# A fused attention and two-MLP kernel: seven products instead of eight in one more stage, and an issue order for the sums at the end of attention

## Chip, cores and metric

One core of one Trainium2 chip. The metric is the device time of one execution in microseconds (us). Five engines are spoken of: PE (TensorE; its weight loads are a row of their own, PEld), DVE (VectorE), ACT (ScalarE), POOL (GpSimd), and SP, which issues the DMAs.

## The reference

Clustered attention feeds an MLP with a squared ReLU, and that feeds a second MLP with a gated activation. There are 1536 tokens (2 batches of 768), model width 512, inner width 2048.

```python
x = attention(q, k, v, centroids)          # 8 heads of 64, softmax within equal clusters
h = np.maximum(x @ w1_in, 0.0);  x = (h * h) @ w1_out
h = x @ w2_in;  out = (h * np.clip(h + 3.0, 0.0, 6.0) / 6.0) @ w2_out
```

## The kernel before

Every product runs in a split form: an operand x is held as hi (rounded to fp32r) and lo = x - hi, and x @ w is three matmuls, hi·hi, hi·lo and lo·hi. ACT makes hi by a copy, DVE or POOL makes lo by a subtraction.

**Attention** is laid out by hand: a table of places says between which tiles each step stands. Its last steps, `emit_norm`, transpose the reciprocal sums on PE (tile `tn`), multiply on DVE (`xx`, L881), round on POOL (`xh<-xx`, L306) and subtract on POOL (`xl<-xx,xh`, L886). `XH` and `XL` then hold the first MLP's input. Near the end the first token block's hidden layer is already computed (tiles `h`, `rg`, `g`).

**The MLPs** are a list of operations with costs; a planner (`Plan.emit`) picks their order engine by engine from due times. The list and the attention are two hand-ordered parts, and the framework merges them: an operation of the MLP whose inputs are ready can be issued in the middle of the end of attention, as the first `token_sums` are.

The hidden dimension is cut into 8 stages of 512 columns, `st` 0 to 7; stages 4 to 7 are the second MLP. From stage 1 on a stage has four turns (pr, p): a token pair pr (two chunks c of 384 tokens) by a weight half p. A turn is a `quad`, which makes four 128x384 blocks of the hidden layer, with three groups of output matmuls of an earlier chunk between its products, and then the rest of that chunk's output matmuls. Turn 4:00 below is stage 4, pr 0, p 0; it carries the output matmuls of stage 3's last chunk. Turns 3:11, 4:00, 4:01 and 4:10 follow each other.

A plain quad takes four products of two terms, 4 x 12 = 48 matmuls. A seven-product quad (Strassen's scheme in Winograd's form) takes 7 x 6 = 42. It needs sums of the tokens (`token_sums`: u1 to u4, then hi and lo of T2, T3, T4 and of u1, which takes the place of XH, XL of chunk c1), sums of the weights (`weights_in`: 4 combinations on POOL, L1108, and 5 splits of 256 columns instead of one of 512) and sums of the results: three copies from bank to SBUF on ACT (`keep`, L1247) and three additions on DVE (`plus`, L1251). All sums of the tokens are recorded at one line (L1161 before, L1163 after), by turns on DVE and POOL.

In before, stages 1, 2, 3, 5, 6 and 7 use seven products and stage 4 uses eight: the sums of the second MLP's input are made during stage 4. PE's order within the MLPs is that of the list.

Names in the rows: banks `b_4179`, `b_4183`, `b_4187`, `b_4191` are a, b, d, e of `quad`; `b_4195`, `b_4199`, `b_4203` are the output banks; `w_68` and `s_4155` are the two weight sets, `s_4163` and `w_4119` the output weights, `wr` the raw weights (L1051 clamps them), `g_4171` (T2, T3 of pair 0), `gB` (T4), `acc` the accumulator, in which the u's are made in place.

Of the kernel before, what the change touches and what calls it, by code (L numbers as in the profile page):

```python
# [13 lines left out]
ALU = mybir.AluOpType  # L14
# [108 lines left out]
E_XL = "p"  # L123
# [128 lines left out]
def span(name, lo, n):  # L252
    return [(name, c) for c in range(lo // 16, -(-(lo + n) // 16))]
# [3 lines left out]
def cluster_attention_mlp_kernel(  # L257
# [17 lines left out]
    nc = tc.nc  # L275
# [4 lines left out]
    NT = B * S  # L280
    R = S // P
    NJ = H // 2
    HS = S // 2
# [9 lines left out]
    XH = xp.tile([P, NJ, NT], F32R, name="xh")  # L293
    XL = xp.tile([P, NJ, NT], F32R, name="xl")

    def f(ap):
        return ap.bitcast(F32)
# [7 lines left out]
    def pool_round(dst, src):  # L305
        nc.gpsimd.tensor_scalar(dst, src, 1.0, 0.0, op0=ALU.mult, op1=ALU.add)  # L306
# [69 lines left out]
    with ExitStack() as actx:  # L376
# [379 lines left out]
        U_t = {}  # L756
# [113 lines left out]
        def emit_norm(u, half):  # L870
            b, j = units[u]
            rb = rows.pop((u, half))
            t = ps_t.tile([P, 512], F32, tag="t", name="tn")
            for c in range(3):
                nc.tensor.transpose(
                    t[:, c * P : (c + 1) * P], rb[:, c].rearrange("p i d -> p (i d)"), ident
                )
            hs = slice(half * HS, half * HS + HS)
            xs = slice(b * S + half * HS, b * S + half * HS + HS)
            xx = sm_p.tile([P, HS], F32, tag="xx", name="xx")  # L880
            nc.vector.tensor_tensor(xx, t[:, :HS], U_t[u][:, hs], op=ALU.mult)  # L881
            if E_XH == "p":
                pool_round(XH[:, j, xs], xx)
            else:
                nc.scalar.activation(XH[:, j, xs], xx, AF.Copy)
            (nc.gpsimd if E_XL == "p" else nc.vector).tensor_sub(XL[:, j, xs], xx, f(XH)[:, j, xs])  # L886

        early = [None, {}]

        def emit_early(fb, part):  # L890

# [84 lines left out]
    with ExitStack() as mctx:  # L976

        def static(name, n, dt):
            pool = mctx.enter_context(tc.tile_pool(name=name, bufs=1, reuse_waits="tile"))
            return pool.tile([P, n], dt, name=name)  # L980

        TT = 384
        tmp = static("tmp", 5 * TT, F32)
# [4 lines left out]
        acc_f = static("acc", 4 * NT, F32)  # L988
# [11 lines left out]
        NS = FF // FQ  # L1000
        acc = acc_f.rearrange("p (d t) -> p d t", d=4)
        acc1 = acc_f.rearrange("p (b n) -> p b n", n=DM)
        plan = Plan()
        K0, K1 = slice(0, 2), slice(2, 4)
# [14 lines left out]
        def cols(c):  # L1019
            return slice(c * TT, c * TT + TT)  # L1020
# [4 lines left out]
        def ak(ds, c):  # L1025
            return [k for d in range(ds.start, ds.stop) for k in span("acc", d * NT + c * TT, TT)]
# [3 lines left out]
        for st in range(1, 2 * NS):  # L1030
            m, fq = divmod(st, NS)
# [122 lines left out]
        def both(name, o, x, y, ko, kx, ky):  # L1154
            plan_op = {"sub": ("tensor_sub",), "add": ("tensor_add",)}[name][0]
            eng = T_ENG[0]
            T_ENG.append(T_ENG.pop(0))
            e, cost = (nc.gpsimd, {"POOL": 1.08}) if eng == "p" else (nc.vector, {"DVE": 0.75})

            def half(d):  # L1160
                plan.add(cost, lambda: getattr(e, plan_op)(o[:, d], x[:, d], y[:, d]), kx + ky, ko)  # L1161

            half(0)  # L1163
            half(1)

        def token_sums(m, n):
            c0, c1 = 2 * n, 2 * n + 1
            t2, t3, t4 = T2[n], T3[n], T4[n]

            def part(ds, c):  # L1170
                return acc[:, ds, cols(c)], ak(ds, c)

            def sub(o, x, y):
                both("sub", o[0], x[0], y[0], o[1], x[1], y[1])

            if m == 0:
                def whole(o, ds, c):
                    both("add", o[0], f(XH)[:, ds, cols(c)], f(XL)[:, ds, cols(c)], o[1],
                         xk("XH", ds, c), xk("XL", ds, c))

                u1, u2, u3, u4 = part(K0, c1), part(K1, c1), part(K0, c0), part(K1, c0)
                whole(u2, K1, c1)
                whole(u1, K0, c1)
                sub(u3, u2, u1)
                whole(u4, K0, c0)
                sub(u1, u1, u4)
                sub(u2, u2, u1)
                whole(u4, K1, c0)
                sub(u4, u4, u2)
            else:  # L1190
                u4, u2, b11, u3 = part(K1, c0), part(K1, c1), part(K0, c0), part(K0, c1)
                if n == 0:
                    u1 = tmp[:, : 2 * TT], [("x", 0), ("x", 1)]
                else:
                    u1 = acc_f[:, 3 * NT : 3 * NT + 2 * TT], span("acc", 3 * NT, 2 * TT)
                u1 = u1[0].rearrange("p (d t) -> p d t", d=2), u1[1]
                sub(u1, u3, b11)
                sub(u3, u2, u3)
                sub(u2, u2, u1)
                sub(u4, u4, u2)  # L1200

            def final(hi, lo, x, hk, lk):
                act(0.92, lambda: nc.scalar.activation(hi, x[0], AF.Copy), x[1], hk)
                both("sub", lo, x[0], f(hi), lk, x[1], hk)

            final(t3.hi, t3.lo, u3, t3.hk, t3.lk)
            final(t2.hi, t2.lo, u2, t2.hk, t2.lk)
            final(t4.hi, t4.lo, u4, t4.hk, t4.lk)
            return lambda: final(
                XH[:, K0, cols(c1)], XL[:, K0, cols(c1)], u1, xk("XH", K0, c1), xk("XL", K0, c1)  # L1210
            )
# [11 lines left out]
        xs = [tmp[:, TT * i : TT * i + TT] for i in range(3)]  # L1223
# [193 lines left out]
        def run(groups):  # L1417
            for g in groups:
                g()
# [75 lines left out]
        for fb in range(NF):  # L1495
            del G[1, fb], G[2, fb]

        laters = []
        for st in range(1, 2 * NS):
            m, fq = divmod(st, NS)  # L1500
            seven = fq > 0

            def turn_of(pr, p, groups, st_out, c):
                some = iter(groups[:3])
                quad(m, pr, p, seven, lambda: next(some)())
                run(groups[3:])
                freed(c)

            weights_in(0, seven)
            if st == 1:  # L1510
                groups = out_groups(0, 3)
            else:
                groups = out_groups(st - 1, 3)
            turn_of(0, 0, groups, st - 1, 3)
            if st == NS:
                laters.append(token_sums(1, 0))
                laters.append(token_sums(1, 1))
            weights_in(1, seven)
            for fb in range(NF):
                weights_out(st, fb)  # L1520
            turn_of(0, 1, out_groups(st, 0), st, 0)
            if laters:
                laters.pop(0)()
            turn_of(1, 0, out_groups(st, 1), st, 1)
            turn_of(1, 1, out_groups(st, 2), st, 2)
            if laters:
                laters.pop(0)()
        run(out_groups(2 * NS - 1, 3))

        with tc.manual_schedule():  # L1530
# [35 lines left out]
```

## Time and profile before

| | us |
|---|---|
| median of 3 runs | 779.55 (778.71 to 780.35) |
| the profiled execution, its own time | 780.98 |
| its span, first to last instruction | 779.2 |
| PE busy | 758.9 (97%) |
| DVE busy | 595.7 (76%) |
| ACT, POOL busy | 498.8, 435.9 |

Attention runs from 0 to about 276, the MLPs from there to the end. The two stretches that the change touches are the seam at 260 to 320 and stage 4 with the turn ahead of it, 497 to 580. A row of the timeline has the start, the length, the engine, the line, the operation with out<-in, and in brackets the engine's idle time just before it and what ended that. A length can hold a wait for a memory port, so a row of the same shape may differ in length. PE's matmuls overlap: the spacing of starts is the rate.

### The profile page before, as it was taken

How to read it: one execution, taken by the hardware profiler on the slowest of the kernel's cores; microseconds unless marked ns; L12 is line 12 of the kernel's file. 1: busy time of each engine (PE TensorE's matmuls, PEld its weight loads, DVE VectorE, ACT ScalarE, POOL GpSimd, SP SyncE). 2: the span in 40 equal slices, each digit the busy share in tenths (PEclk: the TensorE clock that was granted, in tenths of full speed). 3: DMA queues.
4: the chain of work that ended last, by engine and by line, in shares of the span. 5: the costliest groups of instructions: out<-in, count | busy, mean ns of one | idle time of the engine just before them, and what ended most of it. 6: DMA issues, size and time to landing. Idle time of an engine off the chain costs nothing.

```text
span 779.2 us, 12856 instructions
## 1 busy us (share of the span) xinstructions
PE 758.9 (97%) x4402; PEld 716.1 (92%) x4402; DVE 595.7 (76%) x1047; ACT 498.8 (64%) x1059; POOL 435.9 (56%) x544
## 2 busy tenths in 40 slices
PE   7999999999999899999999999999999999999998
PEld 5889999999988799999999999999999889988997
DVE  6789999999998679777768776799546876776444
ACT  4889899998997555774554645655566555464331
POOL 1568788788786758972641643568473164155000
PEclk9899999999999999999999999999999999999999
DMA  8758737638432022231222123122112212300112
GB/s 182 162 113 187 162 87 157 154 82 173 106 75 68 2 63 74 77 113 55 68 95 83 55 63 99 55 66 72 55 55 81 82 55 58 104 28 28 41 40 82
DMA packets 61792, 67.35 MB, mean 86 GB/s; under 512 B 41152, under 2 KB 41408, under 8 KB 61728
## 3 DMA queue, kind: packets, MB, share of 16 engines
q1 hardware_dynamic: 61728, 66.54, 32.5%
q8 instruction: 35, 0.57, 0.3%
q14 instruction: 29, 0.24, 0.1%
HBM read 43.02 MB, written 3.15 MB: 59 GB/s over the span
## 4 chain that ended last, share of the span: by engine, by line
PE 83%; ACT 6%; DVE 6%; DMA 2%; issue 2%; POOL 2%; ACTq 0%; POOLq 0%; SPq 0%; DVEq 0%
PE b L1263 27%; PE b L1379 17%; PE b L1340 15%; PE a L834 7%; PE t L807 6%; PE s L774 3%; PE s L771 3%; ACT e L791 2%; PE tsim L563 2%; PE tq L518 1%; ACT mt L636 1%; DMA op<-HL 1%; DVE acc L1161 1%; ACT eh L817 1%; ACT et L303 1%
## 5 line engine op out<-in xcount | busy, mean ns | idle before, releaser
L807 PE MATMUL t<-ident,e 128*128 128x128 f32 x576 | 94.6, 278 | 7.8 <-ACT e L791 7.0
L1068 POOL TENSOR_TENSOR s<-wt,s 128x512 fp32r<-128x512 f32 (+1 forms) x64 | 66.6, 1051 | 51.3 <-ACT s L1066 42.8
L780 DVE TENSOR_REDUCE nm<-s 128x1 f32<-128x768 f32 x96 | 90.8, 946 | 3.4 <-PE s L774 2.6
L1251 DVE TENSOR_TENSOR b<-b,tmp 128x384 f32<-128x384 f32 x72 | 40.8, 566 | 68.0 <-PE b L1263 36.4
L807 PEld LDWEIGHTS t<-ident,e 128*128 128x128 f32 x576 | 71.6, 142 | 20.0 <-ACT e L791 10.7
L791 ACT ACTIVATE e<-s,nm 128x768 f32<-128x768 f32 x96 | 86.3, 899 | 3.6 <-DVE nm L780 3.2
L1051 POOL TENSOR_SCALAR wr<-wr 128x512 f32<-128x512 f32 x60 | 40.8, 681 | 82.2 <-DMA wr<-in_moe_w_in_dram 51.1
L1247 ACT ACTIVATE tmp<-b 128x384 f32<-128x384 f32 x72 | 35.4, 492 | 79.8 <-PE b L1263 79.7
L815 POOL TENSOR_TENSOR el<-et,eh 128x384 fp32r<-128x384 f32 x80 | 81.9, 1023 | 6.7
L1263 PE MATMUL b<-xh,w 128*128 128x384 f32 x256 | 74.3, 336 | 0.0
L1263 PE MATMUL b<-xh,s 128*128 128x384 f32 x256 | 74.3, 336 | 0.0
L834 PE MATMUL a<-eh,vs 128*128 128x384 f32 x192 | 70.6, 368 | 3.2 <-DVE u L848 3.2
L818 DVE TENSOR_TENSOR el<-t,eh 128x384 fp32r<-128x384 f32 x112 | 61.4, 551 | 15.6 <-ACT eh L817 14.2
L1068 POOL TENSOR_TENSOR w<-wt,w 128x256 fp32r<-128x256 f32 (+1 forms) x44 | 40.8, 938 | 56.2 <-ACT w L1066 47.0
L306 POOL TENSOR_SCALAR eh<-et 128x384 fp32r<-128x384 f32 x80 | 42.5, 532 | 50.1 <-ACT et L303 47.0
L834 PE MATMUL a<-el,vs 128*128 128x384 f32 x192 | 65.3, 340 | 0.0
L817 ACT ACTIVATE eh<-t 128x384 fp32r<-128x384 f32 x112 | 54.8, 491 | 12.3 <-PE t L807 10.6
L1238 ACT ACTIVATE tmp<-b,three 128x384 f32<-128x384 f32 x64 | 37.2, 581 | 35.3 <-DVE b L1251 20.6
L771 PE MATMUL s<-op 128*128 128x384 f32 x192 | 57.5, 382 | 0.0
L1379 PE MATMUL b<-s,gA 128*128 128x512 f32 (+1 forms) x234 | 56.1, 382 | 0.0
L1340 PE MATMUL b<-gA,s 128*128 128x384 f32 x276 | 54.2, 334 | 0.0
L1055 DVE TENSOR_SCALAR b<-wr 128x512 int32<-128x512 int32 x60 | 41.3, 688 | 15.2 <-ACT wr L1054 14.6
(213 smaller groups left out, 2135.4 us busy)
## 6 DMA issues: line engine op xcount, KB each, us to landing
wr<-in_moe_w_out_dram SPq DMA_DIRECT2D x32, 512.0 KB, 3.3
op<-HL SPq DMA_DIRECT2D x84, 192.0 KB, 4.6
wr<-in_moe_w_in_dram SPq DMA_DIRECT2D x28, 512.0 KB, 3.6
rawv<-in_v_dram SPq DMA_DIRECT2D x16, 192.0 KB, 3.7
out_dram<-acc SPq DMA_DIRECT2D x11, 256.0 KB, 2.1
rawq<-in_q_dram SPq DMA_DIRECT2D x14, 192.0 KB, 4.4
rawk<-in_k_dram SPq DMA_DIRECT2D x14, 192.0 KB, 3.9
wr<-in_moe_w_in_dram SPq DMA_DIRECT2D x8, 256.0 KB, 2.9
```

The costliest lines, as they stand in the source:

```text
L771: nc.tensor.matmul(s[:, h, :HS], o[:, 0, rs], o[:, 2, hs], start=True, stop=False)
L780: nc.vector.tensor_reduce(nm, S_t[n][:, :, :HS], axis=AX.XY, op=ALU.max, negate=True)
L791: nc.scalar.activation(e, s[:, :, :HS], AF.Exp, bias=nm, accum_out=sums[u][:, i * R + r : i * R + r + 1])
L807: nc.tensor.transpose(t[:, c, :], E_t[n][:, half, c * P : (c + 1) * P], ident)
L815: nc.gpsimd.tensor_sub(el, et, f(eh))
L817: nc.scalar.activation(eh, t, AF.Copy)
L818: nc.vector.tensor_sub(el, t, f(eh))
L834: nc.tensor.matmul(a[:, :HS], vs[:, kr, i, :], x[:, kr, :], start=(kr == 0 and x is eh), stop=(kr == R - 1 and x is el),)
L1068: pool(n / 365, lambda: nc.gpsimd.tensor_sub(lo, x, f(hi)), k + hk, lk)
L1263: nc.tensor.matmul(h, w[:, a, cc], x[b][:, cc], start=(first and n == 1), stop=(n == 6 * len(terms)), skip_group_check=not first,)
L1340: nc.tensor.matmul(o, x[:, ds], y, start=(fb == 0 and k == 0), stop=(fb == NF - 1 and k == 2))
L1379: nc.tensor.matmul(o, g[:, ts], w[:, ns], start=(fb == 0 and k == 0), stop=(fb == NF - 1 and k == 2),)
```

## The change

Stage 4 takes seven products (`seven = True` in every stage). `token_sums(1, 0)`, of chunks 0 and 1, is listed at the end of stage 3 (behind turn 3:11), `token_sums(1, 1)` behind turn 4:00; before, both stood there and their last step, u1 into XH and XL, came behind later quads. u1 is now made in place in `acc` and no longer in a tile of its own. Every sum of tokens gets an issue order: it stands behind the last `xx` on DVE, or behind the last `xl<-xx,xh` on POOL.

```diff
-            nc.vector.tensor_tensor(xx, t[:, :HS], U_t[u][:, hs], op=ALU.mult)
+            ending["DVE"] = nc.vector.tensor_tensor(xx, t[:, :HS], U_t[u][:, hs], op=ALU.mult)
...
-            (nc.gpsimd if E_XL == "p" else nc.vector).tensor_sub(XL[:, j, xs], xx, f(XH)[:, j, xs])
+            ending["POOL"] = nc.gpsimd.tensor_sub(XL[:, j, xs], xx, f(XH)[:, j, xs])
...
+            def emit(d):
+                with tc.issue_after(ending["DVE" if e is nc.vector else "POOL"].ins):
+                    getattr(e, plan_op)(o[:, d], x[:, d], y[:, d])
...
-                u4, u2, b11, u3 = part(K1, c0), part(K1, c1), part(K0, c0), part(K0, c1)
...
-                sub(u1, u3, b11)
+                u4, u2, u1, u3 = part(K1, c0), part(K1, c1), part(K0, c0), part(K0, c1)
+                sub(u1, u3, u1)
...
-            seven = fq > 0
+            seven = True
...
             if st == NS:
-                laters.append(token_sums(1, 0))
-                laters.append(token_sums(1, 1))
+                token_sums(1, 1)()
...
-            if laters:
-                laters.pop(0)()
+            if st == NS - 1:
+                token_sums(1, 0)()
```

The order of SP's DMAs is the same in both. POOL at the seam, before: four sums stand between the last steps of attention (`g`, `eh`, `el`, then `xh`, `xl` of the last normalisation).

```order
L1051 TENSOR_SCALAR wr_4147<-wr_4147 128x512
L1161 TENSOR_TENSOR acc<-xh,xl 128x384 x2
L1051 TENSOR_SCALAR wr_4151<-wr_4151 128x512
L306 TENSOR_SCALAR g_3716<-rg 128x384
L1161 TENSOR_TENSOR acc<-xh,xl 128x384 x2
L306 TENSOR_SCALAR eh<-et 128x3x128
L815 TENSOR_TENSOR el<-et,eh 128x3x128
L306 TENSOR_SCALAR xh<-xx 128x384
L886 TENSOR_TENSOR xl<-xx,xh 128x384
L306 TENSOR_SCALAR xh<-xx 128x384
L886 TENSOR_TENSOR xl<-xx,xh 128x384
```

POOL at the seam, after.

```order
L1052 TENSOR_SCALAR wr_4147<-wr_4147 128x512
L306 TENSOR_SCALAR g_3716<-rg 128x384
L306 TENSOR_SCALAR eh<-et 128x3x128
L815 TENSOR_TENSOR el<-et,eh 128x3x128
L306 TENSOR_SCALAR xh<-xx 128x384
L886 TENSOR_TENSOR xl<-xx,xh 128x384
L306 TENSOR_SCALAR xh<-xx 128x384
L886 TENSOR_TENSOR xl<-xx,xh 128x384
L1163 TENSOR_TENSOR acc<-xh,xl 128x384 x2
L1052 TENSOR_SCALAR wr_4151<-wr_4151 128x512
L1163 TENSOR_TENSOR acc<-xh,xl 128x384 x2
```

The four sums and one clamp of raw weights have moved behind the last `xl`.

DVE at the seam, after; `u` is the last addition of attention, `xx` its normalisation, `b` and `g` the gating of the first hidden blocks.

```order
L881 TENSOR_TENSOR xx<-tn,u 128x384 x2
L1163 TENSOR_TENSOR acc<-xh,xl 128x384
L1236 TENSOR_TENSOR b_4179<-tmp,b_4179 128x384
L1163 TENSOR_TENSOR acc<-xh,xl 128x384
L1243 TENSOR_TENSOR g_4139<-b_4179,g_4139 128x384
L1236 TENSOR_TENSOR b_4183<-tmp,b_4183 128x384
L1163 TENSOR_TENSOR acc<-xh,xl 128x384
```

The first `acc<-xh,xl` here stood ten rows ahead of `xx` before; the other rows are in their old order, and nothing else of DVE moved until stage 3.

ACT where turn 3:11 ends and 4:00 begins, before: `xh<-acc` are the input's hi parts, `tmp<-b_4179,three` the gate of the first block of stage 4.

```order
L1066 ACTIVATE s_4155<-wt_4175 128x512
L1355 ACTIVATE xh<-acc 128x384 x4
L1238 ACTIVATE tmp<-b_4179,three 128x384
L1242 ACTIVATE s_4159<-b_4179 128x384
L1203 ACTIVATE g_4171<-acc 128x768
L1238 ACTIVATE tmp<-b_4183,three 128x384
L1054 ACTIVATE wr_4151<-wr_4151 128x512
L1242 ACTIVATE gB<-b_4183 128x384
L1238 ACTIVATE tmp<-b_4187,three 128x384
L1203 ACTIVATE g_4171<-acc 128x768
```

ACT at the same place, after.

```order
L1203 ACTIVATE g_4171<-acc 128x768
L1067 ACTIVATE s_4155<-wt_4175 128x512
L1355 ACTIVATE xh<-acc 128x384 x3
L1203 ACTIVATE gB<-acc 128x768
L1247 ACTIVATE tmp<-b_4179 128x384
L1067 ACTIVATE w_68<-wt_4127 128x256
L1247 ACTIVATE tmp<-b_4187 128x384
L1067 ACTIVATE s_4163<-wt_4123 128x512
L1355 ACTIVATE xh<-acc 128x384
```

T3's and T2's hi parts (`g_4171<-acc`) now stand ahead of turn 4:00, and T4's (`gB<-acc`) directly ahead of the first `keep` (`tmp<-b_4179`), which empties bank a.

## Rows read from the trace of the kernel before

**Rows 1.** Waits of PE, 255 to 330: waiter, releaser, us in total, times, longest.
```profile
PE a L834 <- DVE u L848: 3.2, 1, 3.2
```

**Rows 2.** Stretches: length, busy (count) of PE, PEld, DVE, ACT, POOL, PE clock, DMA.
```profile
497.66:513.26 15.60, 15.60 (x92) 15.60 (x91) 10.93 (x20) 9.68 (x20) 9.13 (x10) 1.00 0.11 35
513.26:529.93 16.67, 16.67 (x98) 16.67 (x97) 15.57 (x26) 10.20 (x19) 12.43 (x14) 1.00 0.31 94
529.93:546.61 16.68, 16.68 (x85) 15.14 (x85) 15.49 (x24) 10.55 (x19) 14.89 (x14) 1.00 0.21 65
563.28:579.92 16.64, 16.64 (x85) 15.16 (x85) 8.00 (x14) 10.54 (x21) 10.37 (x14) 1.00 0.19 64
579.92:595.55 15.63, 15.63 (x80) 14.13 (x79) 9.78 (x18) 10.33 (x21) 8.77 (x11) 1.00 0.17 47
```

**Rows 3.** Chain that ended last, in order of time: start, us, engine, tile, line, count.
```profile
271.74 3.01 PE a L834 x12
...
513.26 2.08 PE b L1263 x12
```

**Rows 4.** Timeline of POOL at the seam.
```profile
265.53 1.98 POOL L1161 TENSOR_TENSOR acc<-xh,xl 128x384 f32<-128x384 f32 x2
...
268.19 0.51 POOL L306 TENSOR_SCALAR g<-rg 128x384 fp32r<-128x384 f32 x1
268.67 2.26 POOL L1161 TENSOR_TENSOR acc<-xh,xl 128x384 f32<-128x384 f32 x2
...
283.75 1.29 POOL L1068 TENSOR_TENSOR s<-wt,s 128x512 fp32r<-128x512 f32 x1 [3.66 <-ACT s L1066]
```

**Rows 5.** Timeline of ACT at the seam: the input of `g`.
```profile
265.18 0.53 ACT L365 ACTIVATE rg<-rg 128x384 f32<-128x384 f32 x1
```

**Rows 6.** Timeline of DVE at the seam.
```profile
268.74 1.34 DVE L370 TENSOR_TENSOR g<-rg,g 128x384 fp32r<-128x384 f32 x1 [4.27 <-POOL g L306]
270.00 1.01 DVE L818 TENSOR_TENSOR el<-t,eh 128x384 fp32r<-128x384 f32 x2
271.04 0.55 DVE L848 TENSOR_TENSOR u<-a,tmp 64x384 f32<-64x384 f32 x1
...
275.93 1.02 DVE L881 TENSOR_TENSOR xx<-tn,u 128x384 f32<-128x384 f32 x2
...
277.33 1.28 DVE L1161 TENSOR_TENSOR acc<-xh,xl 128x384 f32<-128x384 f32 x1
...
286.39 0.55 DVE L1243 TENSOR_TENSOR s<-b,s 128x384 fp32r<-128x384 f32 x1
```

**Rows 7.** Timeline of PE behind its wait: full spacing again, and its next wait.
```profile
276.86 0.33 PE L1438 MATMUL b<-xl,w 128*128 128x384 f32 x1
...
287.00 0.45 PE L1438 MATMUL b<-xh,w 128*128 128x384 f32 x1 [0.27 <-DVE s L1243]
```

**Rows 8.** Stretches behind PE's wait, columns as in rows 2.
```profile
274.50:275.60 1.10, 1.10 (x7) 1.07 (x6) 0.25 (x1) 0.49 (x1) 0.00 (x0) 0.50 0.00 0
276.80:278.00 1.20, 1.20 (x9) 1.20 (x8) 1.20 (x3) 0.49 (x1) 1.12 (x2) 1.00 0.00 0
```

**Rows 9.** Timeline of DVE: a sum of tokens with POOL idle.
```profile
313.25 0.55 DVE L1161 TENSOR_TENSOR acc<-xh,xl 128x384 f32<-128x384 f32 x1
```

**Rows 10.** Groups by shape, 497 to 640: count, busy, mean ns of one, idle before.
```profile
L1247 ACT ACTIVATE tmp<-b 128x384 f32<-128x384 f32 x15 | 7.4, 492 | 12.3 <-PE b L1263 12.3
L1108 POOL TENSOR_TENSOR wt<-wt,wt 128x256 f32<-128x256 f32 x10 | 7.4, 738 | 0.5
L1068 POOL TENSOR_TENSOR w<-wt,w 128x256 fp32r<-128x256 f32 x10 | 7.2, 738 | 2.2 <-ACT w L1066 2.2
L1068 POOL TENSOR_TENSOR w<-wt,w 128x512 fp32r<-128x512 f32 x4 | 5.2, 1297 | 5.7 <-ACT w L1066 5.7
L1203 ACT ACTIVATE gB<-acc 128x768 fp32r<-128x768 f32 x2 | 1.7, 836 | 0.0
```

**Rows 11.** Timeline of POOL in turn 3:10's end: the lo parts of chunk 1.
```profile
495.77 4.13 POOL L1356 TENSOR_TENSOR xl<-acc,xh 128x384 fp32r<-128x384 f32 x4 [1.31 <-ACT xh L1355]
```

More of the change, by code (lines that the diff above doesn't have):

```diff
@@ L885, in emit_norm @@
                 nc.scalar.activation(XH[:, j, xs], xx, AF.Copy)
-            (nc.gpsimd if E_XL == "p" else nc.vector).tensor_sub(XL[:, j, xs], xx, f(XH)[:, j, xs])
+            ending["POOL"] = nc.gpsimd.tensor_sub(XL[:, j, xs], xx, f(XH)[:, j, xs])
         early = [None, {}]
+        ending = {}
         def emit_early(fb, part):
@@ L1158, in both @@
             e, cost = (nc.gpsimd, {"POOL": 1.08}) if eng == "p" else (nc.vector, {"DVE": 0.75})
+            def emit(d):
+                with tc.issue_after(ending["DVE" if e is nc.vector else "POOL"].ins):
+                    getattr(e, plan_op)(o[:, d], x[:, d], y[:, d])
             def half(d):
-                plan.add(cost, lambda: getattr(e, plan_op)(o[:, d], x[:, d], y[:, d]), kx + ky, ko)
+                plan.add(cost, lambda: emit(d), kx + ky, ko)
             half(0)
@@ L1190, in token_sums @@
             else:
-                u4, u2, b11, u3 = part(K1, c0), part(K1, c1), part(K0, c0), part(K0, c1)
[L1192 to L1196, printed above, removed]
-                sub(u1, u3, b11)
+                u4, u2, u1, u3 = part(K1, c0), part(K1, c1), part(K0, c0), part(K0, c1)
+                sub(u1, u3, u1)
                 sub(u3, u2, u3)
@@ L1496, in cluster_attention_mlp_kernel @@
             del G[1, fb], G[2, fb]
-        laters = []
         for st in range(1, 2 * NS):
             m, fq = divmod(st, NS)
-            seven = fq > 0
+            seven = True
             def turn_of(pr, p, groups, st_out, c):
@@ L1521, in cluster_attention_mlp_kernel @@
             turn_of(0, 1, out_groups(st, 0), st, 0)
-            if laters:
-                laters.pop(0)()
             turn_of(1, 0, out_groups(st, 1), st, 1)
             turn_of(1, 1, out_groups(st, 2), st, 2)
-            if laters:
-                laters.pop(0)()
+            if st == NS - 1:
+                token_sums(1, 0)()
         run(out_groups(2 * NS - 1, 3))
```

## The prediction

> **What bounds the kernel now.** I read the waits of PE first, then the busy time by stretch, the chain, and last the timelines of the two places that the change touches. From the seam on, PE is the bound: in the turns around stage 4 it is busy for the whole of every stretch (15.60 of 15.60, 16.67 of 16.67) [rows 2], so a matmul that is left out there comes off the end of the kernel, unless something new makes PE wait. At the seam PE has one long wait, 3.2 us for the addition `u` on DVE [rows 1]. The other engines have room on the average but not everywhere: DVE is busy 15.57 of 16.67 in turn 4:00 and 15.49 of 16.68 in 4:01 [rows 2]. These two turns are where the change puts new work.
>
> **Part 1: 24 matmuls fewer.** Stage 4 has four quads, and each loses 48 - 42 = 6 matmuls. Twelve take 2.08 us [rows 3], so 24 take 4.16. A second reading: a turn of stage 4 takes 16.64, a turn of stage 5, which has the same output work and seven products, 15.63 [rows 2]; four times the difference is 4.04. I take 4.1.
>
> What seven products cost beside PE, for each quad: three `plus` on DVE at 0.55, the length of the addition `u` of the same width (1.65) [rows 6], and three `keep` at 0.49 on ACT [rows 10], which has some 6 us free in each turn [rows 2]. For each weight half, POOL gets four combinations at 0.738 and five lo parts at 0.738 in place of one at 1.297, 5.3 more [rows 10]. The sums of tokens are the same in number on each engine as before, but their deadline is a stage earlier: T3 of pair 0 is read by the second product of turn 4:00, where nothing of stage 4 needed a sum before.
>
> **Part 2: the seam.** POOL's row explains PE's wait. `g` starts at 268.19, though its input `rg` landed at 265.18 + 0.53 = 265.71 [rows 4, 5]: two sums and a clamp stood ahead of it. DVE, in its own order, stood still 4.27 us for `g` [rows 6], then did two `el` and `u`, and PE started at 271.74 [rows 3]. With the sums behind `xl`, `g` can start at 265.75 and end at 266.26. DVE's `g` then takes 0.85 to 1.34 (1.34 is the row beside POOL's sum, 0.85 an estimate of it undisturbed), the two `el` 1.0 and `u` 0.55 [rows 6], and PE starts 0.15 later, as before: 268.8 to 269.3, so 2.4 to 2.9 earlier. `eh` on POOL follows `g` after its own input and isn't last. A wait of about 0.8 stays.
>
> The wait has a second price. At 274.5 to 275.6 PE's granted clock is 0.50, the lower of its two levels (1.2 GHz), and at 276.8 it is 1.00 again [rows 8]; PE had been idle for over 3 us ahead of that. The twelve matmuls behind the wait took 3.01 instead of 2.08 [rows 3]. If the short wait leaves the clock up, `xx` on DVE, which follows these matmuls, comes 0.9 earlier still: 3.3 to 3.8 in all. PE itself would be 4.2 ahead by 276.86: 2.4 or more, and from 271.74 to 276.86 (5.12 us) [rows 3, 7] sixteen matmuls at 0.173 (2.77) and six short transposes, which I estimate at 0.6, leave 1.75 that is the clock's.
>
> But PE can't keep 4.2. Its next wait, at 287.00, is for DVE's `s`, which ends at 286.94 [rows 6, 7], and the stretch of DVE from `xx` (275.93) to there is one row of work without a gap; PE waited only 0.27, so it is the tighter of two about equal chains. DVE starts it 3.3 to 3.8 earlier and does one more operation in it, the sum that stood before attention's end: 0.55 alone [rows 9], 1.28 beside POOL's `xl` [rows 6]. So 2.0 to 3.2 arrive, and PE waits more at that point than before, by about 1.5. POOL's four sums (1.98 + 2.26) and the clamp fall into its idle 3.66 us ahead of 283.75 [rows 4]; they overrun it by some 0.3 once everything has moved up, which the next DMA landing absorbs. From there to the first stage the rows are in their old order and move up together. I take **2.7**; the ends are 1.1 (the clock falls all the same, and the moved sum is at its longest: 2.4 - 1.28) and 4.2 (DVE doesn't hold PE).
>
> **Part 3: new waits at stage 4.** No row of before shows PE waiting there, so this is bounded. Over turns 3:11, 4:00 and 4:01 DVE is busy 10.93 + 15.57 + 15.49 = 42.0 [rows 2]. Two seven-product quads add 3.3: 45.3, in a time that shrinks from 48.95 to 46.9. POOL has 9.13 + 12.43 + 14.89 = 36.45 [rows 2], and 10.7 more for the two weight halves is 47.1 of 46.9. POOL is full, then; what saves it is that the last sums are only read 2.6 us or more into turn 4:10, and that some clamps can stand later.
>
> Of the single deadlines the tightest is on ACT. T4's hi part now stands directly ahead of the first `keep` of turn 4:00. It waits for POOL's sum u4, and PE's third product needs the `keep`. That product comes 1.04 + 1.04 + 0.52 = 2.6 after 513.26 (six matmuls, six and a group of three, at 0.173), so u4 is due at 2.6 - 0.84 - 0.49 = 1.3 into the turn, 514.5 (0.84 and 0.49 for the two copies [rows 10]). POOL's row from 495.77 [rows 11] to the second half of u4 holds four `xl`, two lo of u1, two of T2, four sums, all at 1.03 (a quarter of 4.13), and five pieces at 0.738: 12.4 + 3.7 = 16.1, so 511.9 without a wait, and about 513 with the 1 us of waits for ACT that I find in its order. There is 1.5 of slack. DVE's deadlines (T3's lo, then T4's) come out 2 us early, and the later ones about 1. I take **0.6** for what slips, between 0 and the whole 4.1. Below nothing it can't go: PE is busy all through these turns.
>
> A row shows what can stretch all this. A sum on DVE takes 0.55 with POOL idle and 1.28 beside a POOL instruction [rows 6, 9]. The Trainium skill, in "SBUF — State Buffer", section "Who interferes with whom", says that a DVE instruction with two SBUF inputs and a GpSimd instruction that reads SBUF block each other, the second waiting for the first's whole length. The trace agrees (1.28 is below 0.55 + 1.03). By that rule a fuller POOL makes the sums on DVE longer, which speaks against this change; it is the second rival.
>
> **The sum.** Against the profiled execution's own 780.98: - 4.1 - 2.7 + 0.6 = 774.8. That execution lies 1.43 above the median of the timed runs, 779.55, so the forecast is **773.3**.
>
> **The rivals.**
> 1. PE keeps the whole of the seam: DVE's stretch turns out shorter because its sums no longer meet POOL's, and no new wait comes. - 4.2 - 4.1 gives 772.7, as a median 771.2. Against it: DVE's row has no gap to give.
> 2. The memory port. In the three turns DVE does 16 half sums and lo parts of tokens. If all meet POOL (1.28) and not half of them (0.92), DVE has 16 x 0.36 = 5.8 more, of which its spare 1.5 takes some: 4.3 reach PE, and the stage gives nothing. 780.98 - 2.7 - 4.1 + 4.3 = 778.5, as a median 777.0. For it: DVE at 97%. Against it: not every late row of DVE holds PE.
> 3. The change doesn't do at the seam what it says: the sums move, but DVE's continuous row to 287 is as long as before with one more sum in it, or PE's wait passes to another input. Only part 1 with its slip: 780.98 - 4.1 + 0.6 = 777.5, as a median 776.0. Against it: the input `rg` is there 2.5 before `g` starts.
> 4. Slower: POOL becomes the bound of turns 3:11 to 4:10. Its 47.1 is counted with mean lengths. If they are 20% longer because DVE holds the port, 56.5 against 46.9 makes u4, T2 and the weights' lo parts 9.6 late: 780.98 - 6.8 + 9.6 = 783.8, as a median 782.4. It decides from 6.8 us late, that is from lengths 14% over the means. Against it: the means are already from busy stretches.
>
> **How the numbers follow.** Forecast 0.60, rival 1 0.12, rival 2 0.13, rival 3 0.10, rival 4 0.05. The forecast's own terms reach from 771.2 (4.2 + 4.16) to about 775.5 (1.1 and 0.6 slipped); with rival 3 and the near side of rival 2 the range is 771.2 to 776.8. A measurement can tell some 0.2%, 1.6 us, from no change, so faster means below 778.0: all cases but rival 4 and the far side of rival 2. Faster 0.90, same 0.05, slower 0.05.
>
> **What would show it.** Right: PE's wait for `u` shrinks to about 0.8 and the clock stays 1.00 behind it; a new wait of 1 to 2 us on DVE comes near 284; the first quad of stage 1 starts 2.7 earlier; the turns of stage 4 take 15.6 each, with no PE wait over 0.5. Wrong: PE waits for DVE `plus` or ACT `keep` in 4:00 and 4:01 (rival 2), waits that end with POOL (rival 4), or an `xx` that isn't earlier (rival 3).

## The result, and the profile after

The changed kernel takes 773.12 us (median of six runs, 772.24 to 773.31); the kernel before, run beside it, 779.94 (778.71 to 780.38). The ratio is 0.9913, with a 95% interval of 0.9901 to 0.9926. The forecast was 773.3, and faster. The profiled execution of after took 772.61 by its own time and has a span of 770.8; that of before 780.98 and 779.2.

The waits of PE in the stretch from 255 to 340, as in [rows 1]: engine, what waited, what released it, us in total, times, longest.

```profile
PE b L1438 <- DVE s L1243: 2.1, 1, 2.1
PE a L834 <- DVE u L848: 0.2, 1, 0.2
```

Before has three waits under 0.5 there that [rows 1] does not show. One is the 0.27 for `s` in [rows 7]; the other two, behind it, are these:

```profile
PE b L1340 <- ACT acc L1350: 0.4, 1, 0.4
PE b L1462 <- ACT acc L1471: 0.3, 1, 0.3
```

The wait of 3.2 us for `u` has shrunk to 0.2, and that for DVE's `s`, the lo part of the first MLP's third hidden block, has grown from 0.27 to 2.1. The two for ACT's copies are gone. From 480 to 600 the trace lists no wait of PE at all. There the stretches by turn, columns as in [rows 2], in the order 4:00, 4:01, 4:10, 4:11 and last 3:11:

```profile
509.11:524.73 15.62, 15.62 (x91) 15.62 (x91) 12.35 (x23) 12.38 (x26) 14.53 (x19) 1.00 0.14 38
524.73:540.38 15.65, 15.65 (x80) 14.11 (x79) 14.52 (x24) 10.35 (x19) 15.62 (x15) 1.00 0.31 98
540.38:556.00 15.62, 15.62 (x79) 14.12 (x79) 10.66 (x19) 9.47 (x18) 4.86 (x6) 1.00 0.01 2
556.00:571.61 15.61, 15.61 (x80) 14.13 (x79) 10.25 (x19) 10.83 (x23) 9.80 (x13) 1.00 0.32 100
493.50:509.11 15.61, 15.61 (x92) 15.61 (x91) 13.12 (x23) 10.42 (x22) 15.45 (x17) 1.00 0.11 35
```

Every turn of stage 4 lasts 15.6 instead of 16.7 [rows 2], and PE is busy throughout. POOL is busy 15.62 of 15.65 in turn 4:01 and 15.45 of 15.61 in 3:11: it is nearly as full as forecast, and PE does not notice.

At the seam, POOL's and DVE's rows (start, length, engine, line, operation, in brackets the idle time ahead and what ended it), to be read beside [rows 4, 6]:

```profile
263.94 0.51 POOL L306 TENSOR_SCALAR g<-rg 128x384 fp32r<-128x384 f32 x1 [0.25 <-ACT rg L365]
...
274.53 2.30 POOL L1163 TENSOR_TENSOR acc<-xh,xl 128x384 f32<-128x384 f32 x2
276.92 0.65 POOL L1052 TENSOR_SCALAR wr<-wr 128x512 f32<-128x512 f32 x1
```
```profile
264.49 0.56 DVE L370 TENSOR_TENSOR g<-rg,g 128x384 fp32r<-128x384 f32 x1 [1.86 <-POOL g L306]
...
270.24 1.02 DVE L881 TENSOR_TENSOR xx<-tn,u 128x384 f32<-128x384 f32 x2
271.18 0.62 DVE L1163 TENSOR_TENSOR acc<-xh,xl 128x384 f32<-128x384 f32 x1
...
278.31 0.70 DVE L1056 TENSOR_SCALAR b<-wr 128x512 int32<-128x512 int32 x1 [0.79 <-ACT wr L1055]
...
281.77 0.55 DVE L1243 TENSOR_TENSOR s<-b,s 128x384 fp32r<-128x384 f32 x1
```

POOL starts `g` 0.07 after the end of `rg` (263.34 + 0.53) where it was 2.5 after it (0.25 is POOL's own idle time ahead of `g`), and DVE's idle time ahead of its own `g` falls from 4.27 to 1.86. DVE's row from `xx` to `s` was without a gap before [rows 6]; now it has one of 0.79. DVE's `g` itself takes 0.56 instead of 1.34; before has as short a one for an earlier block:

```profile
252.83 0.56 DVE L370 TENSOR_TENSOR g<-rg,g 128x384 fp32r<-128x384 f32 x1 [0.47 <-POOL g L306]
```

The chain of work that ended last (start, us, engine, tile, line, count) says what the gap is made of:

```profile
266.71 2.35 PE a L834 x12
...
274.53 2.30 POOL acc L1163 x2
...
276.92 0.66 POOL wr L1052
...
277.60 0.68 ACT wr L1055
...
278.31 0.71 DVE b L1056
...
281.77 0.56 DVE s L1243
```

The twelve matmuls take 2.35 where they took 3.01 [rows 3], and the granted clock is 1.00 from 264 to 282: it held there. But the chain then passes through the two sums that the change put behind `xl`, since the second clamp of raw weights stands behind these on POOL; ACT scales what was clamped, DVE decodes it, and `s` stands behind the decoding. The prediction had this clamp in POOL's idle time.

For all further comparisons I use two marks that every profile has: the start of attention's last `rg` on ACT, and the start of stage 1's first lo part on DVE. For before and for after:

```profile
336.52 0.56 DVE L1243 TENSOR_TENSOR s<-b,w 128x384 fp32r<-128x384 f32 x1
```
```profile
263.34 0.53 ACT L365 ACTIVATE rg<-rg 128x384 f32<-128x384 f32 x1
...
332.37 0.56 DVE L1243 TENSOR_TENSOR s<-b,w 128x384 fp32r<-128x384 f32 x1
```

From the second mark to the end of the span before has 779.2 - 336.52 = 442.68 and after 770.8 - 332.37 = 438.43. The difference, 4.25, is what 24 matmuls take (4.16 by [rows 3]). Between the marks ("the seam") before has 336.52 - 265.18 = 71.34 [rows 5] and after 69.03, so 2.31 less. The remaining 1.84 of the 8.4 between the spans lies ahead of the first mark, in attention, where the change has nothing; run e11 below shows what 1.1 of it was.

### The profile page after: what moved, and what is told of

It reads as the page before. It is cut to its first block, busy times and chain, and to the rows that moved or that the text cites. A ratio compares the mean times of both kernels' runs of the same rounds, so it can differ in the third digit from the quotient of the medians.

```text
span 770.8 us, 12850 instructions
## 1 busy us (share of the span) xinstructions
PE 751.7 (98%) x4378; PEld 709.3 (92%) x4378; DVE 599.5 (78%) x1059; ACT 505.8 (66%) x1079; POOL 448.3 (58%) x560
## 4 chain that ended last, share of the span: by engine, by line
PE 85%; ACT 6%; DVE 5%; issue 2%; DMA 1%; POOL 1%; SPq 0%; ACTq 0%; POOLq 0%
PE b L1263 27%; PE b L1379 17%; PE b L1340 16%; PE a L834 6%; PE t L807 6%; PE s L774 3%; PE s L771 3%; ACT e L791 2%; PE b L1438 2%; PE tsim L563 2%; PE tq L518 1%; DMA op<-HL 1%; DVE nm L780 1%; PE b L1462 1%; ACT mt L636 1%
## 5 line engine op out<-in xcount | busy, mean ns | idle before, releaser
L1251 DVE TENSOR_TENSOR b<-b,tmp 128x384 f32<-128x384 f32 x84 | 47.6, 566 | 62.4 <-PE b L1263 39.6
L1247 ACT ACTIVATE tmp<-b 128x384 f32<-128x384 f32 x84 | 41.3, 492 | 83.4 <-PE b L1263 83.1
L1069 POOL TENSOR_TENSOR s<-wt,s 128x256 fp32r<-128x256 f32 (+1 forms) x68 | 69.0, 1023 | 37.5 <-ACT s L1067 29.8
L1069 POOL TENSOR_TENSOR w<-wt,w 128x256 fp32r<-128x256 f32 (+1 forms) x48 | 43.0, 906 | 68.3 <-ACT w L1067 57.1
L306 POOL TENSOR_SCALAR eh<-et 128x384 fp32r<-128x384 f32 x80 | 42.6, 532 | 48.3 <-ACT et L303 45.3
L1263 PE MATMUL b<-xh,w 128*128 128x384 f32 x224 | 66.2, 336 | 0.0
L1263 PE MATMUL b<-xh,s 128*128 128x384 f32 x224 | 66.2, 336 | 0.0
```

Source lines behind the costliest of these rows:

```text
L1069: pool(n / 365, lambda: nc.gpsimd.tensor_sub(lo, x, f(hi)), k + hk, lk)
L1263: nc.tensor.matmul(h, w[:, a, cc], x[b][:, cc], start=(first and n == 1), stop=(n == 6 * len(terms)), skip_group_check=not first,)
```

## The experiments

The seam is the time between the two marks, the rest that from the second mark to the end of the span, both from the profiled execution. Medians and ratios are of the timed runs; the ratio's denominator is the kernel before beside it.

| run | median us | ratio (95%) | seam | rest |
|---|---|---|---|---|
| before | 779.94 | | 71.34 | 442.68 |
| e11, before again | 781.01, one run | | 72.44 | 442.68 |
| after | 773.12 | 0.9913 (0.9901 to 0.9926) | 69.03 | 438.43 |
| e5, after again | 773.36 | 0.9915 (0.9900 to 0.9929) | 69.05 | 438.44 |
| e1, order only | 777.03 | 0.9954 (0.9940 to 0.9967) | 70.04 | 442.59 |
| e2, seven only | 776.18 | 0.9940 (0.9927 to 0.9953) | 72.05 | 438.47 |
| e3, early clamp | 772.95 | 0.9901 (0.9888 to 0.9915) | 68.63 | 438.48 |
| e4, clamp and DVE's sums | 772.21 | 0.9893 (0.9880 to 0.9907) | 68.79 | 438.25 |
| e10, e4 again | 771.50 | 0.9890 (0.9876 to 0.9904) | 68.25 | 438.28 |
| e6, all sums held | 780.34 | 0.9994 (0.9983 to 1.0004) | 75.28 | 438.42 |
| e9, six sums first | 771.15 | 0.9885 (0.9869 to 0.9900) | 67.25 | 438.30 |
| e12, e9 again | 770.95 | 0.9888 (0.9871 to 0.9905) | 67.07 | 438.29 |
| e7, u4 two operations later | 773.97 | 0.9918 (0.9903 to 0.9933) | 69.06 | 439.15 |
| e8, u4 six operations later | 779.26 | 0.9991 (0.9981 to 1.0000) | 69.03 | 444.23 |

**The two parts alone.** e1 is the kernel before with the issue order of the change and nothing else; e2 is the changed kernel without it. The edit of e1, against before:

```diff
...
+            def emit(d):
+                with tc.issue_after(ending["DVE" if e is nc.vector else "POOL"].ins):
+                    getattr(e, plan_op)(o[:, d], x[:, d], y[:, d])
...
```

The edit of e2, against after:

```diff
-                with tc.issue_after(ending["DVE" if e is nc.vector else "POOL"].ins):
-                    getattr(e, plan_op)(o[:, d], x[:, d], y[:, d])
+                getattr(e, plan_op)(o[:, d], x[:, d], y[:, d])
```

> Part 2 of the change alone: the kernel before with its sums of tokens ordered behind the end of attention's normalisation; stage 4 keeps eight products. Theory (the two parts add up, and the seam gives some 2.3 us, which is what the two profiles leave for it): about 777.5 us beside about 779.9 for the kernel before, ratio 0.997; the last twelve matmuls of attention wait less than 0.5 us for u and run at a granted clock of 1.00. Rival (the seam's gain is given back before stage 1 ends, and all of the change's gain is the 24 matmuls): 779.9, ratio 1.000. Rival (the seam carries most of it): 775 or less.

> Part 1 of the change alone: stage 4 with seven products, the sums of tokens left to the scheduler as before. Theory: 24 matmuls of 0.172 us go and nothing comes in their place: 4.1 us less, about 775.7 us, ratio 0.9947; the wait for u at the seam is 3 us or more again, with the clock at 0.50 behind it, and stage 4's four turns last 15.6 us each. Rival (the sums of stage 4 arrive late by the 0.6 us that the prediction gave them): about 776.3. Rival (the new order was needed for the seven products, too): 779 or more.

The parts are separate in the profile: only e2 has the short rest (438.47, with no wait of PE at stage 4), only e1 the short seam. By the medians e1 is 780.58 - 777.03 = 3.55 faster than the kernel before beside it, e2 4.40, together 7.95; after and e5 gain 6.8 to 7.0. The intervals cover that difference (0.14% either way is 1.1 us for each), so the parts add up as far as can be told, and neither needs the other. That e1 gave more by the median than its profile shows at the seam is no contradiction: its profiled execution was the slowest of its five (778.00). Its seam is 1.0 longer than after's, and one row says why:

```profile
281.43 1.73 DVE L1163 TENSOR_TENSOR acc<-acc 128x384 f32<-128x384 f32 x1
283.09 0.54 DVE L1248 TENSOR_TENSOR s<-b,s 128x384 fp32r<-128x384 f32 x1
...
283.69 0.44 PE L1443 MATMUL b<-xh,w 128*128 128x384 f32 x1 [3.26 <-DVE s L1248]
```

The sum directly ahead of `s` took 1.73 here and 0.55 in after, and PE waited 3.26 instead of 2.07. It meets POOL's lo part `s<-wt,s`, whose row is in e1 and then in after:

```profile
281.47 1.28 POOL L1069 TENSOR_TENSOR s<-wt,s 128x512 fp32r<-128x512 f32 x1
```
```profile
281.33 1.65 POOL L1069 TENSOR_TENSOR s<-wt,s 128x512 fp32r<-128x512 f32 x1
```

In both kernels the two instructions start within 0.04 us of each other (in after DVE's sum at 281.30). In after POOL's took 0.37 more and DVE's ran at full speed; in e1 POOL's ran at its usual 1.28, and DVE's took 1.18 more. The Trainium skill ("SBUF — State Buffer", "Who interferes with whom") says that a DVE instruction with two SBUF inputs contends with a GpSimd instruction that reads SBUF, and that issue order decides which of two contending ones blocks. The trace agrees that either of them can be the one that pays. Which of the two was issued first it does not show: by the starts DVE's is ahead in both kernels, by 0.03 and 0.04 us.

**What binds after the change.** In e3 the second clamp runs in POOL's idle time directly behind attention's last `el`, ahead of the sums. In e4, in addition, DVE's first sums stand behind the third `s`.

```diff
+            def clamp_late():
+                with tc.issue_after(ending["EL"].ins):
+                    clamp()
...
+            pool(0.70, clamp_late if n == 1 else clamp, [rh], [rh])
...
+                behind = hold.get("p" if e is nc.gpsimd else "v")
+                if behind is not None:
+                    plan.before[-1].add(behind)
...
```

`hold["p"]` is that clamp; in e4 `hold["v"]` is the lo part of the third gated block. A sum that has one of them in `before` can't be planned ahead of it. Both kernels also list the output weights of the first two blocks ahead of the sums (e6 and e9 those of all four), and the planner's order changes with that: in e3 two of the four sums that POOL has ahead of its first two `s<-wt,s` in after slid behind these.

> The changed kernel, with one step moved: the second clamp of the raw weights on GpSimd (wr_4151, 128x512) runs directly behind attention's last el there instead of behind the first two sums of tokens. Theory (after the change the first gated row is bound by VectorE's waiting 0.79 us for ScalarE's product, which waits for this clamp): the 0.79 us gap goes, TensorE's wait for the first s falls from 2.07 to about 1.3 us, and the time is 0.5 to 2 us below the changed kernel's 773.1 (2 if the granted clock then no longer falls behind that wait). Rival (the row is bound by VectorE's own work, the gap only moves): wait 2.0, time within 0.5 us of the changed kernel. Rival (the clamp in that place delays el's readers or ScalarE, so that the row starts later): 0.3 to 1 us slower than the changed kernel.

> As the run before it (clamp moved ahead), and VectorE's first sums of tokens held behind the third gated block's s, so that the first two s stand ahead of them on VectorE. Theory: the moved sum (0.62 us) and the gap (0.79 us) both leave VectorE's row between xx and the first s; TensorE's wait of 2.07 us there shrinks below 1 us, the granted clock does not fall behind it (0.80 and 0.85 in the two stretches of the changed kernel's profile), and the time is 1 to 2.5 us below the changed kernel's. Rival (the clock falls behind any such wait, the length does not matter): 1 us at most. Rival (held sums come late for the first transform of stage 0, and TensorE waits there for its tokens instead): same as the changed kernel or slower.

> The kernel of run e4 once more. Theory (e4 is 0.1 to 0.2 percent faster than the changed kernel, since two falls of the clock and two waits became one of each): ratio 0.989 to 0.990 of the kernel before, beside 0.9913 and 0.9915 for the changed kernel. Rival (the difference was noise): 0.991 or above.

PE's waits from 255 to 340 beside the one of 0.2 for `u`, first in e3, then in e4:

```profile
PE b L1352 <- ACT acc L1362: 1.6, 1, 1.6
PE b L1450 <- DVE s L1255: 1.5, 1, 1.5
```
```profile
PE b L1476 <- POOL s L1076: 1.8, 1, 1.8
```

e3 confirms the cause: DVE's gap of 0.79 is gone, the wait for `s` falls from 2.07 to 1.46, by 0.61, and the clock does not fall behind it. The wait shrinks by less than the gap because DVE's sum directly ahead of `s` took 0.83 there and 0.55 in after. But a wait of 1.64 for ACT's copy `acc` comes later, near 312, and the time does not move beyond the scatter (0.9901 beside 0.9913, where 0.5 to 2 us less was expected). The copy stands behind ACT's scaling of raw weights, and that waits for a clamp on POOL, which waits for a DMA:

```profile
308.57 0.94 POOL L1054 TENSOR_SCALAR wr<-wr 128x512 f32<-128x512 f32 x1 [2.51 <-DMA wr<-in_moe_w_in_dram]
```

In e4 the wait for `s` is gone, and POOL's lo part of the output weights, which stands behind sums there, takes its place with 1.78. The repetition e10 has 1.67 there and 0.85 for the copy. Both runs of e4's kernel lie under both of after's, by about 0.2%; the intervals overlap.

**All sums out of the way.** In e6 all of stage 0's sums, on both engines, stand behind the decoding of the fourth block of output weights.

```diff
-        later = token_sums(0, 0)
         for fb in range(NF):
             weights_out(0, fb)
+        hold["p"] = splits[3]
+        hold["v"] = decodes[3]
+        later = token_sums(0, 0)
```

> The changed kernel with the early clamp of the run e3, and all sums of tokens of stage 0, on both engines, held behind the decode and split of the fourth block of output weights. Theory (in the seam every wait of TensorE that is left comes from weight decode queued behind sums on VectorE and GpSimd): the waits for s (2.07 in the changed kernel, 1.78 for GpSimd's s in the run e4) both fall below 0.5 us, the granted clock stays at 1.00 from 270 to 325 us, and the time is 2 to 4 us below the changed kernel, 769 to 771. Rival (the sums are needed by stage 1's first quad and come late now: GpSimd was 4.00 of 4.00 busy from 282 to 302 us): the wait reappears at stage 1, between 300 and 335 us, and the time is the changed kernel's or up to 3 us above it.

PE's two long waits, and ACT's rows at the first of them:

```profile
PE b L1476 <- ACT acc L1485: 3.1, 1, 3.1
PE b L1354 <- ACT acc L1364: 2.8, 1, 2.8
```
```profile
293.82 0.49 ACT L1485 ACTIVATE acc<-b 128x384 f32<-128x384 f32 x1 [1.75 <-DVE g L1173]
295.11 0.49 ACT L1485 ACTIVATE acc<-b 128x384 f32<-128x384 f32 x1 [0.79 <-DVE g L1173]
```

All that the change had won was lost (780.34, ratio 0.9994): 7.0 more than e5 beside it, where the rival allowed 3. The theory that only weight decoding was late fell: the sums are made in `acc`, and the copy of the first output block must write there. It waited until DVE had subtracted `g` from `acc` (released by DVE `g`), PE waited for the bank that this copy empties, and the seam took 75.28.

**Between the two.** e9 is e4 with POOL's first six sums where they were and the others behind the split of the fourth output block, so that the wait of 1.78 should go without the copy's coming late.

```diff
+                if e is nc.gpsimd and behind is not None:
+                    first[0] -= 1
+                    if first[0] < 0:
+                        behind = splits[3]
```

> The kernel of run e4 (early clamp, VectorE's first sums behind the third s), and on GpSimd the sums from the seventh on stand behind the split of the fourth block of output weights, which in e4 waited on GpSimd behind sums and kept TensorE 1.78 us. Theory (that wait and the clock's fall behind it go, and sums held by so little do not come late): the wait for GpSimd's s at 291 falls below 0.8 us, the granted clock stays at 1.00, and the time is 1 to 3 us below e4's, ratio 0.985 to 0.988. Rival (what e6 showed: the sums are kept in the accumulator that the first output block's copy writes, so each delayed sum delays that copy): the wait moves to the copy acc at 294 or to the one at 312, 1 to 2 us long, and the ratio is e4's 0.989 or above.

> The kernel of run e9 once more, on another chip if it falls so. Theory (it is the fastest version, some 2 us below the changed kernel): ratio 0.987 to 0.989 of the kernel before, and again a wait of 1 to 2 us for the copy acc near 310 as the only one of TensorE at the start of the second MLP beside 0.2 us for u. Rival (the difference to the changed kernel's 0.9913 and 0.9915 was noise): 0.990 or above.

The same of e9, then of e12:

```profile
PE b L1360 <- ACT acc L1370: 1.5, 1, 1.5
```
```profile
PE b L1360 <- ACT acc L1370: 1.1, 1, 1.1
```

This is the fastest version: 771.15 and 770.95, some 0.3% under after (e9's interval ends at 0.9900, where e5's begins; e12's reaches into those of after and e5), with a seam of 67.25 and 67.07. Against e4's kernel it gained 1.0 to 1.7 at the seam, but only 0.35 by the median of e10, which ran beside it (771.50), less than the 1 to 3 expected. The wait that is left is that of the copy near 310, as the rival said. In e9's ACT row the copy stands behind the scaling of raw weights (`wr`, released by POOL's clamp), and the clamp ran as soon as its DMA had landed:

```profile
307.14 0.88 POOL L1054 TENSOR_SCALAR wr<-wr 128x512 f32<-128x512 f32 x1 [1.16 <-DMA wr<-in_moe_w_in_dram]
...
308.05 0.68 ACT L1062 ACTIVATE wr<-wr 128x512 f32<-128x512 f32 x1 [1.79 <-POOL wr L1054]
308.62 0.62 ACT L1074 ACTIVATE w<-wt 128x512 fp32r<-128x512 f32 x1
309.14 1.23 ACT L1370 ACTIVATE acc<-b 128x384 f32<-128x384 f32 x3
```

Whether another order of ACT there would give the last 1 to 1.5 us was not tried.

**The slack at stage 4.** The prediction gave part 3 a price of 0.6, because the last sum u4 had 1.5 us of slack by its count. e7 and e8 delay that sum by two and by six subtractions on POOL. The edit of e7, against after (e8 has `* 3`):

```diff
                 sub(u4, u4, u2)
+                if n == 0:
+                    for d in [0, 1] * 1:
+                        plan.add({"POOL": 0.01}, lambda d=d: nc.gpsimd.tensor_sub(
+                            u4[0][:, d], u4[0][:, d], u2[0][:, d]), u4[1] + u2[1], u4[1])
```

> The changed kernel with two more subtractions of 128x384 on GpSimd behind the last sum of tokens (u4 of the first two columns) before stage 4, which makes that sum ready some 2.0 to 2.7 us later, and its values wrong: a test of the slack there. Theory (u4's reader on ScalarE, the copy to gB, runs at 509.36, 0.55 us behind u4, and TensorE wants the block queued behind it at 511.70, 0.7 to 1.0 us behind its end): TensorE waits 0.5 to 1.7 us in the first turn of stage 4, and the time rises by 0.5 to 2 us over the changed kernel. Rival (the waits are taken up by the products queued ahead): the same time, within 0.3 us.

> As the run before it, with six more subtractions instead of two: u4 is ready 6 to 8 us later. Theory (what lies beyond the slack of about 1 to 1.5 us is paid in full): TensorE waits 4 to 6.5 us in the first turn of stage 4, plus a fall of the granted clock behind it, and the time rises by 4 to 8 us. Rival (GpSimd becomes the bound of stage 4 altogether, since it had hardly a gap from 488 to 545 us, and the delay is paid a second time by the sums of the other two columns): the rise is above 8 us. Rival (all of it is hidden): the rise is below 2 us.

POOL's added rows and PE's wait, in e7 and then in e8, and last PE's clock (the third number from the end) in the stretch behind e8's wait:

```profile
511.00 1.98 POOL L1203 TENSOR_TENSOR acc<-acc 128x384 f32<-128x384 f32 x2
...
514.29 1.34 PE L1267 MATMUL b<-g,w 128*128 128x384 f32 x6 [0.39 <-ACT tmp L1251]
```
```profile
509.52 5.80 POOL L1203 TENSOR_TENSOR acc<-acc 128x384 f32<-128x384 f32 x6
...
516.63 2.29 PE L1267 MATMUL b<-g,w 128*128 128x384 f32 x6 [4.21 <-ACT tmp L1251]
```
```profile
516.60:518.00 1.40, 1.37 (x4) 1.37 (x5) 1.40 (x2) 1.07 (x3) 1.32 (x2) 0.50 0.00 0
```

Both give the same slack. The sum came 512.98 - 511.03 = 1.95 later in e7, and PE waited 0.39, a little less than expected: 1.56 was free. In e8 it came 515.32 - 509.55 = 5.77 later (509.55 is the end of POOL's row ahead of the added ones), and PE waited 4.21: again 1.56. By the starts of PE's matmuls, which overlap, the delay is 0.17 more (in e7 from 513.22 to 514.29, where after has 511.03 to 511.54), and the slack 1.4. Both waits are for ACT's `tmp`, which is the `keep` behind `gB<-acc`, the chain that the prediction named. e8's rest is 444.23 - 438.44 = 5.79 longer: the wait, and 1.6 more with the clock at 0.50 behind it. By the medians it is 5.9. POOL's six operations were paid once; no second wait came from the sums of the other two columns, so POOL, though busy for 54.13 of the 57 us from 488 to 545 in after, did not become the bound.

**The kernel before, once more.**

> The kernel before once more, for a second profile of it. Theory (the granted clock of 0.50 from 18 to 22 us, behind a wait of 1.28 us for a DMA, belonged to that one execution and explains 1.5 us of the 8.4 us between the two profiles): no such fall now, the last rg of attention at 263 to 264.5 instead of 265.18, a span of 777 to 778.5, and at the seam again a wait of 3.2 us with 71.3 us from that rg to the first s<-b,w of stage 1. Rival (the kernel before always starts so): rg at 265 again, span 779.

Its rest is 442.68 again, its `rg` comes at 264.08 (before: 265.18), and the clock of 0.50 from 18 to 22 us is not there. First the wait ahead of it and the stretch in the first profile of before, then the stretch in e11:

```profile
15.69 0.97 PE L774 MATMUL s<-op 80*128 80x384 f32 x4 [1.28 <-DMA op<-HL]
```
```profile
18.00:22.00 4.00, 3.62 (x15) 3.52 (x16) 3.02 (x9) 2.69 (x8) 1.51 (x2) 0.50 1.01 217
```
```profile
18.00:22.00 4.00, 2.75 (x18) 2.45 (x19) 3.83 (x11) 3.49 (x9) 1.52 (x2) 1.00 0.98 221
```

So 1.1 of the late `rg` was that execution's. The other 0.74 to after is scatter: in the twelve profiles without that fall `rg` comes between 263.20 and 264.49. The rest of the expectation missed: the span is 779.2 again, not 777 to 778.5, because e11 lost 1.1 more at the seam (72.44). There the clock fell sooner behind the same wait of 3.18 (the row of PE, and the stretch behind it):

```profile
270.65 0.41 PE L834 MATMUL a<-eh,vs 128*128 128x384 f32 x1 [3.18 <-DVE u L848]
```
```profile
270.60:272.00 1.40, 1.35 (x5) 1.38 (x6) 1.06 (x2) 0.27 (x1) 0.81 (x1) 0.62 0.00 0
```

In the first profile the clock was still 1.00 through 272 to 273 and fell at 273. From PE's first matmul behind the wait to the second `u` it took 275.35 - 271.74 = 3.61 there, 275.15 - 270.65 = 4.50 in e11 and 269.66 - 266.71 = 2.95 in after, without a fall. e2, which has the old seam, is like e11 (4.45).

**After, once more.**

> The changed kernel once more, on the chip of the next three runs. Theory: about 0.991 of the kernel before; its profile shows TensorE waiting some 2 us for the first s of stage 0, and the first s<-b,w of stage 1 on VectorE some 69 us behind the last rg of attention (71.34 in the kernel before). Rival (the 2.07 us wait and the fall of the clock behind it were one execution's): the wait is 1 us or less.

The seam repeats to 0.02 us (69.05), the wait for `s` to the hundredth (2.07), and the fall of the clock behind it, though it begins later: from 282.80 to 285 the mean is 0.80 and from 285 to 287 it is 0.50, while in the first profile of after it is at the lower level from the first matmul on:

```profile
282.37 0.67 PE L1438 MATMUL b<-xh,w 128*128 128x384 f32 x1 [2.07 <-DVE s L1243]
282.84 0.52 PE L1438 MATMUL b<-xl,w 128*128 128x384 f32 x1
...
285.96 0.52 PE L1438 MATMUL b<-xh,w 128*128 128x384 f32 x2
```

Eleven matmuls lie between the first and the last of these rows, 3.59 us; at 0.173 [rows 3] they would take 1.90. The fall costs 1.7. e7 and e8, whose edit is at stage 4 only, have the same wait of 2.07 and seams of 69.06 and 69.03.

## Why the prediction held, step by step

- **What bounds.** Right. PE is the bound from the seam on, and a matmul left out comes off the end: the rest shrinks by 4.2 to 4.4 in every kernel with seven products (but for e7 and e8, which delay a sum there), and by 0.09 in e1.
- **Part 1, -4.1.** 4.25 by the marks, 4.40 by e2's median. The second reading (a turn of stage 5) was as good as the count: the turns last 15.6.
- **Part 2, -2.7.** The size held, in part by luck: parts of it were wrong and cancelled. By the medians the seam gave 6.8 - 4.25 = 2.6 in after and 3.55 in e1; by the marks 2.31 against the first profile of before and 3.4 against e11. The steps: PE's start was to be 2.4 to 2.9 earlier with a wait of about 0.8 left (0.3 to 0.8 by these numbers); it came 3.2 earlier against `rg` (271.74 - 265.18 = 6.56 before, 266.71 - 263.34 = 3.37 after), and the wait was 0.2. The term that was too large is DVE's `g`: it took 0.56, under both of the lengths considered (0.85 and 1.34), with no sum beside it. Before had shown as short a one at 252.83. The clock stayed up, as said. The new wait on DVE was there, 2.07 for a forecast of about 1.5 more than before's 0.27, at 282.37 for "near 284", with attention 1.84 earlier. At the end of this wait PE was 2.79 earlier against `rg` (287.00 - 265.18 = 21.82 before, 282.37 - 263.34 = 19.03 after). What the prediction did not see is the clamp: it put sums and clamp together into POOL's idle time and counted an overrun of 0.3, but not that ACT and DVE want the clamp's result ahead of POOL's own next step. That is the gap of 0.79 (e3, without it: 0.61 less of the wait). Nor did it see that the clock would fall behind the new wait (1.7). Of that 1.7 the seam lost only 2.79 - 2.31 = 0.48: the two waits for ACT's copies (0.4 and 0.3) are not in after; what made up the other 0.5 is open.
- **Part 3, +0.6.** It cost nothing: no profile with seven products shows a wait of PE at stage 4, but for those of e7 and e8. The count of the slack was nearly exact (1.5 said, 1.4 to 1.56 measured). The mistake was to price at 0.6 a step that its own count put inside the slack; 0 was the nearer end. The count of DVE's time was off: 45.3 of 46.9 said for turns 3:11 to 4:01, 13.12 + 12.35 + 14.52 = 39.99 measured. 17 rows of weight decoding there (L1055 to L1060) became 13, and 15 sums and lo parts of tokens 13. POOL's 47.1 came out at 45.60.
- **The sum.** 774.8 was set against the profiled execution. The forecast for the median, 773.3, took off the 1.43 by which that execution lay above the median of three runs. That it came within 0.2 of 773.12 is in part luck. The gain was 6.82 and not the 6.2 of the sum, and the 0.6 between them is the size of part 3; but the kernel before, run beside after, took 779.94 and not 779.55, 0.4 the other way. Nor is the 1.43 the late `rg` alone: e11, without it, took 781.01. The upper end of the forecast's own terms was added up wrongly: 779.55 - 4.1 - 1.1 + 0.6 is 774.95, not 775.5. The range does not hang on it.
- **The rivals.** 1 (PE keeps the seam, 771.2): e9 comes near it, but only with three more moves, so DVE and POOL did hold PE, as argued. 2 (the port): the sums on DVE in turns 3:11 to 4:01 took 0.55 to 1.38, but on the average no more than before (0.97 in both), though POOL was fuller, and no late row held PE. 3 (nothing at the seam): ruled out by e1. 4 (POOL the bound): ruled out in this kernel. e8 shows what lateness there costs: nothing up to the slack, and 5.77 late took back 5.9 of the change's 7.0.

## What to carry over

Where an engine's queue is in order, put what feeds the next engine's chain ahead of what is only needed later, and do it for the whole chain: moving four sums behind attention freed 3.2 us, and a 0.65 us clamp left behind two of them took some of it back on three engines. A sum that lives in the accumulator has a due time of its own, the copy that wants its place; held too long, it made the seam 6 us longer (75.28 against 69.03). A slack counted row by row held here (1.5 against 1.4 to 1.56): price a step at zero when it fits, and test it by delaying that very operation.

## What the hardware showed that was not expected

- The granted clock fell to 0.50 behind waits of PE of 1.78 (e4), 2.07 (after, e5, e7 and e8), 2.8 and 3.1 (e6), 3.2 (before, e11, e2, e1) and 4.2 us (e8), and not behind 1.46 (e3), 1.5 (e9 and e11), 1.63 (e2), 1.64 (e3) and 1.67 (e10). In before and e7, the two profiles with a wait of 1.28 or 1.29 at the start of attention, it also fell there, 1.4 and 2.7 us behind that wait; the other profiles wait 1.03 or less there, and it did not fall. At the seam the fall began with the first matmul behind the wait in after and e2, 0.3 us later in e11, 1.3 in e5, 1.4 in before and 1.5 in e1. What decides this is open.
- Two executions of the same kernel with the same wait (3.18) differ by 0.9 us at the seam (3.61 and 4.50 from the wait's end to the second `u`), and what differs there is when the fall begins. One profile of such a place is a sample.
- Two instructions of DVE and POOL that start within 0.04 us of each other can come out either way: DVE's sum ahead of `s` took 0.55 in after and 1.73 in e1, and PE's wait behind it was 2.07 and 3.26.
- Gain does not add up along a wait: e3 took 0.61 of wait and a fall of 1.7 away and won 0.4 at the seam, because another wait, of 1.64 for the copy behind a DMA, came in its place.
